# A level of a matrix inverse, copied and transposed in two halves of a PSUM pair

## The chip, the core and the metric

The kernel runs on one core of a Trainium2 chip. The metric is the device time of one execution in microseconds (us). Engines are named as in the profile: PE is TensorE (matmuls; PEld is its weight loads), DVE is VectorE, ACT is ScalarE, POOL is GpSimd, SP is SyncE, which issues all DMAs here.

## The reference

Two parts follow on each other. The first is a linear recurrence over 768 steps for 4 batches of 8 heads with 40 channels; the state of each is 40x40. Its output, with the heads laid side by side as 3072 tokens of 320 channels, is the input of a feed-forward part with 2048 inner channels.

```python
for t in range(S):
    y[:, :, t] = np.einsum('bhd,bhde->bhe', rt, state)
    Sa = np.einsum('bhde,bhe->bhd', state, at)
    state_decay = state * wt[:, :, None, :] - np.einsum('bhd,bhe->bhde', Sa, bt)
    state = state_decay + np.einsum('bhd,bhe->bhde', vt, kt)
...
h = x @ w_in
g = h * (1.0 / (1.0 + np.exp(-1.702 * h)))
return (g @ w_out).astype(np.float32)
```

All numbers are 32-bit floats.

## The kernel before

**Units.** Time is cut into 12 chunks of 64 steps, and a chunk's 32 pairs of batch and head into two units of 16; there are 24 units, two for each chunk. Within a unit the recurrence over 64 steps is solved as a triangular system: products of the inputs give score matrices (`ps_A`, `ps_N`, `ps_RV`), a triangular matrix has to be inverted (`inverse`, L662), and the inverse T is applied (`ps_X`, masked into M at L907), from which y and the next state are read (`ps_y`, L913). Two finished units of a chunk are scaled, sent through DRAM and come back as the input of the feed-forward part (`mlp`, L975: products `ps_up`, a gelu on ACT, products `ps_down`).

**Products.** Every product is a matmul with operands of 64 rows or 40 rows, on one of four 64x64 quarters of the array; four neighbours in `QUARTERS` use the four quarters. An operand of a product that many matmuls share is two PSUM banks, a pair, held as one tile of [128, 2, 512] (`psum`, L294). There are four pairs. `mm` (L299) is the line under which the profile lists all matmuls.

**The inverse.** The matrix of each head is 64x64: two diagonal blocks of 32, which are inverted by five levels of repeated squaring and multiplying, and a block below them, which is made afterwards. Units 4 to 23 use `level` (L736): a product `ps_level`, a copy of all of it to W (L751, 512 elements a partition), a subtraction (L753), a transpose (L702) and a spreading (L707, L709). Units 0 to 3 (`PLAIN`) use `plain_level` (L758): the product makes, for each of eight matrices, 96 columns, of which the first 64 are the next power and the last 32 the inverse so far. Then follow

- L784, on ACT in 15 and on DVE in one of the 16: a copy of all 2 x 4 x 96 = 768 columns of the pair to PT, the moving operand of the next level;
- L723 (called at L786), on DVE: a transpose, block by block, of the first 64 of each 96 columns to EX, the stationary operand of the next level.

The last level has 32 columns a matrix only. Behind it (the tail of the inverse):

- L790: its result is transposed into ES (L702), and ES is spread into T (L707 on ACT, in two instructions; POOL or DVE elsewhere), a tile with two places for each row block, the other filled with zeros;
- L797: eight small copies of the result into Tc, four tasks of two;
- L801, `off_one`: the product Q of P21 (the lower block of N, copied at L692) and the lower places of T; all 64 rows enter, of which the upper 32 hold zeros;
- L811: Q is masked into QT; L822, `off_two`: the product T21 of Tc and QT; L830: T21 is added to T, which is then complete for X.

**Order.** Nothing is scheduled at run time. The tasks of a plan are numbered in the order in which they are added, and a long list (`ORDER`, L107) names for every task the engine and, for those on PSUM, the pair: `300p1` is task 300 on PE with pair 1. Each engine works through its own part of the list. The semaphore waits between engines are put in by the framework from what the instructions read and write. ACT's and DVE's parts of the list also hold the conversion of the feed-forward weights (L447 on ACT, L451, L455 and L459 on DVE, L463 on POOL), which arrive as 64-bit integers' bits and fill the first 100 us or so.

Units 0 and 1 are inverted in turn between about 14 and 42 us, units 2 and 3 between about 47 and 90 us.

Of the kernel before, what the change touches and what calls it, by code (L numbers as in the profile page):

```python
# [111 lines left out]
279d 63s 280g 119p3 277s 171d1 36s 44s 123a3 120d3 343s 125d3 121a 278g 124d3 29d 287a 126p2 170a1 288p0 127a2 30d 172p1 122a3
31d 289a0 128p2 54s 173a1 129d2 32g 174d1 134p3 147s 37a 290d0 175p2 135d3 180a2 146s 178a2 275s 176d2 136p1 179a2 479s 38d
181a2 45s 39d 177a 282g 291d 91s 138a1 182p0 188p3 281d 183a0 186p2 139d 137a1 283p0 187a2 184p1 189a3 40d 276s 292p2 46a
284d0 41g 285p3 185d1 344s 148a 286d3 190p0 293a2 294d2 334p1 335p3 357a 140s 191d0 268g 336a3 315d 192p2 47d 337a1 348d 316p0
194a2 295p3 349d 61s 317a0 195g 60s 347s 358p1 296a3 62s 297d3 360d1 318a0 298p3 271a 361d 319p0 338g 300d3 196s 193a2 320a0
346s 355p2 385d 270s 48d 299a3 362p0 356d2 351g 301p3 363a0 364d0 350g 269s 141s 386p2 197s 302d3 365p0 387a2 352g 359a1 303d3
388a2 323p1 367d0 366a0 321p3 49d 324a1 304p2 322a3 478s 325d1 50g 353p0 309a2 470p3 354d0 209p1 307a2 210p1 310a2 305d2 211p1
308a2 272d 198p0 341a 199p0 72s 212p1 70s 64a 200p0 340s 368p2 52s 342d 339s 69s 201p0 369a2 202p0 370d2 203p0 471a 213p1 65d
214p1 389p2 66d 472a3 483g 204p0 390a2 560s 371p3 67d 306a 53s 215p1 71s 482s 216p1 372a3 217p1 476a 220p2 373d3 68g 218p1  # L120
221p2 477d 219a1 205p0 222p2 206p0 223p2 224p2 207p0 55a 311p3 225p2 79s 312d3 80s 226p2 208a0 58d 313p1 374p3 314d1 227p2 56d
379a3 228p2 229p2 57d 326p0 230a2 59g 393p1 327d0 378a3 391p2 394a1 375d3 231p0 558s 392d2 376a 232p0 233p0 395d1 559s 81s 73a
78s 234p0 480s 381p2 235p0 328p1 481s 382a2 74d 377a3 485d 380a3 236p0 75d 492a 242p2 486d 243p2 82a 76d 484d 77g 383p3 237p0
384d3 244p2 329d1 330d1 488p3 473d 238p0 531d 245p2 487g 246p2 489d3 85d 532p1 239p0 533a1 396p3 331d 332s 474s 475s 534a1
240p0 247p2 397d3 562s 241a0 535p1 83d 490p3 536a1 84d 398p0 572a 491d3 86g 550p1 555s 561s 253p3 399d0 551a 333s 400d0 254p3
401d 402s 554s 255p3 552a1 564d 493p0 705s 556a 567g 570p1 403s 494d0 248p2 563d 566g 249p2 495d0 498d 256p3 571d1 565g 250a2
496a0 251d2 252s 696p1 497g 557d 539p0 537p2 704s 257p3 538a2 540d0 258p3 553d 611d 697a 499d 573p2 784s 700s 259p3 576a2
574d2 710d 260p3 541d0 575d2 404p0 578d 261a3 577g 405p0 579d 698a1 568p2 711g 500p1 406p0 569d2 501a1 407p0 262d3 263s 708s
580p2 702a 502d1 408p0 582d2 409p0 503d 410p0 583d 504a 612p3 411p0 584g 613d3 412p0 614d3 413p0 505p1 709d 414a0 426p3 506d1
427p3 428p3 507d1 429p3 699d 581d2 430p3 615p1 785s 706s 701s 703d 431p3 616a1 585p0 432p3 508d 586a0 433p3 587d0 434p3 509a  # L130
588d 435p3 589d 448p2 436a3 510p1 590p0 511a1 449p2 592d0 591a0 512d1 415p3 513d 416p3 593d 514a 417p3 594g 418p3 515p0 419p3
516a0 517d0 595p1 518d 420p3 596a1 597d1 421p3 598d 422p3 519a 599d 423p3 424p3 520p0 425a3 437p1 521d0 438p1 523d0 522g 439p1
524d0 440p1 525d0 441p1 442p1 526d0 527p3 718p0 929s 528a3 443p1 719d0 787s 444p1 720d0 529p3 445p1 721d0 446p1 530d3 600p0
723d 447a1 542p3 722d 724g 603d0 605a0 619p1 604d0 543d3 450p2 620a1 606d0 544p3 621d1 601d0 602d 617p1 707s 546d3 451p2 618a1
783s 712d 547g 713d 607p0 725p1 608a0 452p2 609p0 453p2 548s 610d0 932s 454p2 727d1 726d1 622p0 728d 545d3 729a 775p1 455p2
623d0 780s 776a 549s 756d 730p3 624p0 456d2 457d2 731d3 458s 459p2 777a1 778g 732d3 786s 788g 781a 779s 626d0 460p2 625d0 627g
733d 795p1 835d 734a 461p2 735p3 791g 462p2 628s 736a3 796d1 737d3 716p0 792g 738d 463p2 782d 739g 1011s 920p1 757p3 925s
464p2 717d0 758a3 629s 759a3 790d 465p2 740p0 789d 466p2 741a0 742d0 921a 797p3 467d2 760p0 1008s 468d2 800a3 923d 652p2 469s
761d0 922a1 653p2 926a 930s 798d3 714p1 799d3 654p2 924s 802d 801g 655p2 934d 803a 656p2 836p0 657p2 715d1 658p2 659p2 837d0
762p3 838d0 927d 660p2 763a3 661p2 764p1 662a2 743d 630p0 744d 928s 631p0 632p0 765d1 804p3 766d1 633p0 805a3 806d3 634p0 807d  # L140
635p0 808a 745p2 636p0 748d2 637p0 749d2 839p1 933g 750d2 638p0 840a1 1009s 751d2 639p0 809p3 746d2 935g 640a0 641p1 810d3
642p1 793p2 747a 811d3 674p0 812d 794d2 813a 752p3 643p1 753a3 814p2 644p1 815a2 816d2 754p3 645p1 755d3 646p1 817d 647p1 818a
767p2 841p3 768d2 648p1 842a3 649p1 819p2 650p1 820a2 821d2 675p0 769p3 822d 651a1 823d 771d3 931s 770d3 772g 824p2 936d 676p0
827a2 828a2 942p1 829a2 677p0 1153s 830a2 937d 945a1 773s 663p3 825d2 664p3 943d1 1156s 826a 665p3 944d1 999p2 947d 946g 666p3
1000a 1004s 980d 940p1 948g 667p3 941d1 668p3 774s 669p3 670p3 831p1 671p3 1001a2 1002d 1003s 832d1 672p3 1005a 1013d 678p0
673a3 1006d 833p2 843p1 679p0 834d2 1007s 844d1 938p2 845d1 680p0 939d2 846p3 681p0 847d3 949p1 1012g 682d0 848p2 950a1 683d0
1014d 684s 685p3 849d2 1015g 1010s 850d2 1021p0 1016g 951d1 686p3 1024a0 1232s 851d 1235s 981p2 687p3 982a2 952d 852s 1022d0
983a2 953g 1144p1 1023d0 688p3 1026d 1145a 1149s 1025d 1027g 984p2 1059d 689p3 1154s 954p0 853s 985a2 1147g 690p3 1158d 1148s
955a0 956d0 986p2 1146a1 957d 1150a 691p3 958d 987a2 1151d 988p0 692p3 989a0 1152s 990d0 959p1 693a3 865p2 960a1 694d3 866p2
961d1 867p2 695s 962d 868p2 963d 1028p0 869p2 1029a0 1030d0 870p2 1031d 1157g 871p2 1159d 1032a 1060p3 872p2 873p2 1061a3  # L150
874p2 1062d3 1033p1 875a2 854p0 1035d1 855p0 1036d 856p0 1037d 1063p3 857p0 1064d3 1034a1 858p0 964p2 859p0 965a2 966d2 1038p1
967d 860p0 1039a1 1040d1 861p0 1041d 1017p3 968a 1042g 862p0 1018d3 863p0 969p2 864a0 876p1 970d2 877p1 972d2 971g 1043p3
973d2 878p1 1044a3 974d2 879p1 975d2 880p1 881p1 1045d3 1019p0 1046d 976p2 1047a 882p1 1020d0 1233s 883p1 977a2 1166p3 884p1
1169a3 1167d3 1377s 978p0 885p1 1168d3 898p2 1171d 1170g 886a1 979d0 887p3 1172a 1048p0 991p1 1051a0 888p3 1052a0 992d1 889p3
1053a0 890p3 1054a0 891p3 1049d0 993p1 1050a 1067p0 994d1 1160g 1155s 892p3 1161d 1068a0 893p3 894p3 1069d0 1380s 895p3 1204d
1065p0 995d1 896p3 996d 1066a0 1231s 1055p1 899p2 897a3 1056d1 997s 1173p0 1223p3 900p2 1174a0 1175d0 1228s 1176d 1224a 1177g
1057p1 901p2 1058d1 1070p0 998s 1164p1 1225a3 1226d 1236g 1227s 1071d0 902p2 1229a 1165d1 1162p3 903p2 1238d 1163d3 904p2
1237d 1178p0 1230d 905p2 1179a0 1180d0 1245p1 906a2 1181d 1072p3 1248a1 1456s 907d2 1182g 1246d1 908s 1247d1 909p0 1250d 1234s
1239g 1073d3 1251a 910p0 1240g 1074d3 1249d 1183p2 1459s 1283d 1368p1 911p0 1184a2 1075d 1373s 912p0 1185d2 1369a 1076s 1186d
1252p3 1187d 913p0 1370a1 1371g 1372s 1382d 1253a3 1188p2 1254d3 1374a 914p0 1255d 1190d2 1256g 1077s 1189a2 1191d 1243p1  # L160
1375d 915p0 1192g 1257p3 916p0 1244d1 1258a3 1259d3 1205p2 917d0 1206a2 1193p1 918d0 1207a2 1089p3 1260d 919s 1196a1 1090p3
# [87 lines left out]
def rwkv7_gelu_quick(ctx: ExitStack, tc: tile.TileContext, time_d, v_d, w_d, wc_d, ak_d, b_d, rv_d, w_in, w_out, out):  # L249
    nc = tc.nc  # L250
# [407 lines left out]
    def turn(i, n, of):  # L658
        return of * 2 * (i // 2) + i % 2 + 2 * n
# [470 lines left out]
```

## Time and profile before

| what | value |
|---|---|
| median of 3 runs | 678.3 us (677.63 to 680.24) |
| the profiled execution | 678.87 us |
| its span in the trace | 677.2 us |
| granted PE clock over the span | 0.989 |
| L784 on ACT (768 elements) | 15 times, 800 ns |
| L723 from PSUM (512 elements) | 16 times, 709 ns |
| L751 on ACT (512 elements) | 56 times, 585 ns |
| matmuls of Q | 384 in the trace (two for each), 220 ns |

The span runs from the first to the last instruction; the execution's own time has a little around it. A row of a group gives how often an instruction stands in the trace, its busy time, the mean of one in ns, and the idle time of its engine just before it with what ended that idle time. A matmul's own duration is its way through the array; neighbours overlap, so that a block of 16 takes far less than 16 durations.

### The profile page before, as it was taken

Reading aid. Unit: us, or ns where it says so; the run is one execution under the profiler, and the core shown is the slowest. Engines: PE = TensorE matmul, PEld = TensorE weight load, DVE = VectorE, ACT = ScalarE, POOL = GpSimd, SP = SyncE. Lnnn points to the kernel's source line nnn. Section 1 sums busy time; section 2 is a strip of 40 time slices with the busy share of each in tenths; the row PEclk is TensorE's granted clock in tenths of the full one; section 3 lists DMA queues with packets and bytes.
Section 4 is the critical chain, followed back from the end, with each engine's and each line's share of the span. In section 5 each row is a group of like instructions: output and inputs, shape, how many; then the busy total and the mean of one; then the engine's idle time right before and its main releaser. Section 6 shows DMA issues by size and latency. Waiting matters only on the chain.

```text
span 677.2 us, 42176 instructions
## 1 busy us (share of the span) xinstructions
PE 650.6 (96%) x19488; PEld 561.3 (83%) x19488; DVE 447.1 (66%) x906; ACT 330.6 (49%) x688; POOL 175.0 (26%) x204
## 2 busy tenths in 40 slices
PE   5668999999999999999999999999999999999997
PEld 5567887987987888898998898787988799899895
DVE  5686887777768668667776687868556766675001
ACT  4675955634664655554545435454454354252110
POOL 6442444224123023124123211321412321300000
PEclk9887999999999999999999999999999999999999
DMA  7883736315324224332304413513412412100100
GB/s 234 295 252 126 235 111 183 103 45 157 111 64 132 84 62 129 106 107 77 113 24 133 139 34 108 155 33 107 145 34 72 126 46 63 53 14 29 45 12 20
DMA packets 35311, 69.72 MB, mean 103 GB/s; under 512 B 5440, under 2 KB 14656, under 8 KB 35136
## 3 DMA queue, kind: packets, MB, share of 16 engines
q1 hardware_dynamic: 35136, 67.03, 32.6%
q8 instruction: 153, 2.51, 1.5%
q14 instruction: 22, 0.18, 0.1%
HBM read 59.15 MB, written 7.86 MB: 99 GB/s over the span
## 4 chain that ended last, share of the span: by engine, by line
PE 94%; ACT 2%; DVE 2%; issue 1%; DMA 1%; DVEq 0%; ACTq 0%; SPq 0%
PE ps_up L300 31%; PE ps_down L300 31%; PE ps_level L300 9%; PE ps_y L300 5%; PE ps_B L300 5%; PE ps_X L300 2%; PE ps_A L300 2%; PE ps_rz L300 2%; PE ps_N L300 2%; PE ps_RV L300 2%; PE ps_zT L300 1%; ACT PT L784 1%; PE ps_cum L300 1%; PE ps_Q L300 1%; PE ps_T L300 1%
## 5 line engine op out<-in xcount | busy, mean ns | idle before, releaser
L300 PE MATMUL ps_up<-xT_all,w_sb 64*64 64x256 f32 x3840 | 250.1, 377 | 0.4 <-PE ps_rz L300 0.2
L300 PE MATMUL ps_down<-w_sb,g 64*64 64x320 f32 x3072 | 239.5, 430 | 0.3 <-ACT zr L869 0.2
L300 PEld LDWEIGHTS ps_up<-xT_all,w_sb 64*64 64x64 f32 x3840 | 169.6, 133 | 15.3 <-issue 0.8
L300 PEld LDWEIGHTS ps_down<-w_sb,g 64*64 64x64 f32 x3072 | 133.3, 133 | 39.8 <-issue 1.3
L988 ACT ACTIVATE g<-ps_up 128x1024 f32<-128x1024 f32 x48 | 49.2, 1024 | 45.0 <-PE ps_up L300 44.6
L709 POOL TENSOR_TENSOR EX<-ES,quads 128x512 f32<-128x512 f32 x29 | 38.3, 1323 | 113.3 <-DVE ES L702 75.8
L751 ACT COPY W<-ps_level 128x512 f32<-128x512 f32 x56 | 32.7, 585 | 69.7 <-PE ps_level L300 68.0
L300 PEld LDWEIGHTS ps_level<-W,EX 64*64 64x64 f32 x2560 | 58.7, 134 | 5.8 <-DVE T L830 0.2
L300 PE MATMUL ps_level<-W,EX 64*64 64x64 f32 (+1 forms) x2560 | 55.9, 217 | 0.0
L753 DVE TENSOR_TENSOR E<-two,ps_level 128x256 f32<-128x256 f32 x80 | 33.2, 416 | 34.0 <-ACT W L751 30.3
L707 ACT ACTIVATE EX<-ES,quads 128x256 f32<-128x256 f32 x80 | 36.3, 501 | 30.5 <-DVE ES L702 29.9
L619 POOL TENSOR_TENSOR ak<-ak,FT 128x512 f32<-128x512 f32 x16 | 21.4, 1335 | 75.9 <-DMA ak<-in_ak 52.0
L300 PEld LDWEIGHTS ps_level<-PT,EX 64*64 64x64 f32 x1280 | 32.1, 146 | 8.8 <-DVE EX L723 5.7
L300 PE MATMUL ps_level<-PT,EX 64*64 64x64 f32 (+2 forms) x1280 | 34.2, 245 | 5.3 <-DVE EX L723 4.5
L702 DVE STREAM_TRANSPOSE ES<-E 128x256 f32<-128x256 f32 x80 | 35.3, 443 | 4.4
L300 PE MATMUL ps_y<-M,bh 64*64 64x104 f32 (+1 forms) x768 | 35.0, 247 | 2.4 <-issue 2.1
L300 PE MATMUL ps_y<-RV,kh 64*64 64x104 f32 (+1 forms) x768 | 34.8, 247 | 0.0
L891 ACT COPY B<-ps_B 128x416 f32<-128x416 f32 (+1 forms) x34 | 16.5, 491 | 33.8 <-PE ps_B L300 33.6
L300 PEld LDWEIGHTS ps_y<-RV,kh 64*64 64x64 f32 x768 | 28.5, 133 | 2.3 <-DVE M L907 0.5
L300 PEld LDWEIGHTS ps_y<-M,bh 64*64 64x64 f32 x768 | 27.2, 133 | 2.8 <-issue 2.3
L907 DVE TENSOR_TENSOR M<-ps_X,later 128x832 f32<-128x832 f32 (+1 forms) x24 | 23.8, 993 | 8.2 <-PE ps_X L300 8.0
L627 POOL TENSOR_TENSOR kh<-time,G 128x320 f32<-128x320 f32 x18 | 16.1, 892 | 48.5 <-PE ps_y L300 34.6
(131 smaller groups left out, 1092.9 us busy)
## 6 DMA issues: line engine op xcount, KB each, us to landing
ak<-in_ak SPq DMA_DIRECT2D x48, 160.0 KB
rv<-in_rv SPq DMA_DIRECT2D x48, 160.0 KB
time<-in_time SPq DMA_DIRECT2D x24, 320.0 KB
xT_all<-x_dram SPq DMA_DIRECT2D x48, 160.0 KB
wc<-in_wc SPq DMA_DIRECT2D x20, 264.0 KB
logw<-in_w SPq DMA_DIRECT2D x24, 160.0 KB
RV<-in_v SPq DMA_DIRECT2D x24, 160.0 KB
b<-in_b SPq DMA_DIRECT2D x48, 80.0 KB
```

The lines of the kernel that those rows point to most:

```text
L300: nc.tensor.matmul(o, lhsT, rhs, start=start, stop=True, skip_group_check=True)
L619: plan.add(R, {"DVE": 690.0, "POOL": 1270.0, "sbuf": True}, lambda t: of(t.engine).tensor_mul(ahT(), ahT(), FT_of(i)), reads=T("ak", "FT") ...
L627: plan.add(R + 4, {"POOL": 870.0, "DVE": 490.0, "sbuf": True}, lambda t, n=n, dst=dst: of(t.engine).tensor_mul(dst(i)[:, :, :D], by_head(t ...
L702: plan.add(rank, dve(256), lambda t: nc.vector.transpose(ES(n), source(t)), writes=[key("ES", n, 6)], **reads)
L707: nc.scalar.activation(dst[:, :, h], ES(n), ACT.Copy, scale=quads[:, h, :1])
L709: of(t.engine).tensor_mul(dst, ES(n).unsqueeze(2).to_broadcast([128, 8, 2, 32]), quads.unsqueeze(1).to_broadcast([128, 8, 2, 32]))
L751: plan.add(rank, any2(512), lambda t: copy(t.engine)(tiles_of(W(n + 1)), blocks(psum(t, ""), 64)), writes=[key("W", n + 1, 5)], pair=pair)
L753: plan.add(rank, dve(256), lambda t: nc.vector.tensor_sub(tiles_of(E(n + 1)), every(two32, [128, 2, 4, 32]), blocks(psum(t, ""), 64)[:, :, ...
L784: plan.add(rank, any2(768), lambda t: copy(t.engine)(tiles_of(PT), blocks(psum(t, ""), 96)), writes=[("PV", turn(i, n + 1, 5))], pair=pair)
L891: plan.add(R, any2(4 * wide), lambda t: copy(t.engine)(dst(), some(psum(t, "")[:, :, :208])), writes=[("Bv", i)] if x and c > 0 else T("B" ...
L907: plan.add(R + 1, dve(8 * wide), lambda t: nc.vector.tensor_tensor(M_of(i)[:, :, :wide].rearrange("p (j b) n -> p b j n", b=2), some(psum( ...
L988: plan.add(-45, {"ACT": 1030.0, "table": "gelu"}, lambda t: nc.scalar.activation(g_of(c * NQ + q).rearrange("p m r n -> p r m n"), psum(t, ...
```

## The change

- **Halves.** In `plain_level` the copy of 768 becomes two of 384, one for each bank of the pair (`copied(r)`), and the transpose of 512 two of 256 (`transposed(r)`). They are added in the order: copy of bank 1, transpose of bank 0, transpose of bank 1, copy of bank 0.
- **Trimmed copies.** The last level reads only the last 32 columns of each matrix. The copy ahead of it leaves the others out: 2 x 128 elements instead of 768 in `plain_level`, 256 instead of 512 at L751 (once in each of units 4 to 23).
- **32-row product.** Q reads ES and the lower 32 of each 64 rows of P21, instead of the lower places of T and all 64 rows. It waits for the transpose L702 and no longer for the spreading of T. The tile of its matmuls in the built program is 32x64 instead of 64x64; that of all others stays 64x64.
- **Order.** `ORDER` is written anew for the 32 tasks more. In the built program the instructions of SP and POOL stand as before. On PE only two things differ: the source of Q, and in unit 0 the product N of unit 2, which stood behind Q and now stands behind T21. On ACT the four Tc copies on ACT in unit 0's tail now all stand ahead of QT, and QT ahead of the spreading of T (before: two Tc copies, T, preset, a copy of unit 1, QT, two Tc copies). Some results of units 1 and 2, which DVE transposed ahead of ACT's copy (among them the first of unit 1), now have their copy of bank 1 first. On DVE only the pairs of halves are new.

```diff
+    LOWER = [slice(h.start + 32, h.stop) for h in HALF]
...
-            plan.add(rank, any2(512), lambda t: copy(t.engine)(tiles_of(W(n + 1)), blocks(psum(t, ""), 64)),
+            past = 32 if n == LEVELS - 2 else 0
+            plan.add(rank, any2(512 - 8 * past), lambda t: copy(t.engine)(tiles_of(W(n + 1))[:, :, :, past:], blocks(psum(t, ""), 64)[:, :, :, past:]),
...
-            plan.add(rank, any2(768), lambda t: copy(t.engine)(tiles_of(PT), blocks(psum(t, ""), 96)),
-                     writes=[("PV", turn(i, n + 1, 5))], pair=pair)
-            turned_square(lambda t: blocks(psum(t, ""), 96)[:, :, :, :64], dict(pair=pair), n + 1)
+            past = 64 if n == LEVELS - 2 else 0
+
+            def copied(r):
+                plan.add(rank, any2(384 - 4 * past), lambda t: copy(t.engine)(tiles_of(PT)[:, r, :, past:], blocks(psum(t, ""), 96)[:, r, :, past:]),
+                         writes=[("PV", turn(i, n + 1, 5))], pair=pair)
+
+            def transposed(r):
+                plan.add(rank + 0.5, dve(256), lambda t: nc.vector.transpose(tiles_of(square(n + 1))[:, r], blocks(psum(t, ""), 96)[:, r, :, :64]),
+                         writes=[key("EX", n + 1, 5)], pair=pair)
+            copied(1)
+            transposed(0)
+            transposed(1)
+            copied(0)
...
-                    mm(ps[HALF[u], b, e * 64:e * 64 + 64].rearrange("p (f t) -> p f t", f=2), at(P21_t, i)[HALF[b], 128 * e + 64 * u:128 * e + 64 * u + 64],
-                       at(T_t, i)[HALF[b], j:j + 2, 1], e == 0)
-        plan.add(R + 3.5, pe((2, 64)), off_one, reads=T("P21", "T0"), room=T("QT"), pair=("Q", i))
+                    mm(ps[HALF[u], b, e * 64:e * 64 + 64].rearrange("p (f t) -> p f t", f=2), at(P21_t, i)[LOWER[b], 128 * e + 64 * u:128 * e + 64 * u + 64],
+                       ES(LEVELS)[LOWER[b], j:j + 2], e == 0)
+        plan.add(R + 3.5, pe((2, 64)), off_one, reads=T("P21") + [key("ES", LEVELS, 6)], room=T("QT"), pair=("Q", i))
```

More of the change, by code (lines that the diff above doesn't have):

```diff
@@ L112 @@
[L112 to L115, printed above, removed]
@@ new lines @@
+2606p1 2291p0 2545d3 2546d 2607d1 2547a 2292p0 2548p2 2293a0 2617p3 2549a2 2294d0 2452p1 2618d3 2453p1 2295s 2454p1 2550d2
+2649p0 2551d 2455p1 2650a0 2619d3 2552g 2456p1 2651a0 2620d 2457p1 2621a 2652p2 2458p1 2653d2 2553p3 2459p1 2554a3 2555d3
+2460p1 2556d 2461p1 2557d 2622p0 2462a1 2463p2 2623d0 2464p2 2465p2 2624d0 2558p3 2625d 2466p2 2626d 2559a3 2467p2 2560d3
+2468p2 2561d 2469p2 2562a 2627p0 2470p2 2628d0 2471p2 2472p2 2629d0 2563p1 2630d 2473a2 2474p3 2631d 2475p3 2564d1 2476p3
+2566d1 2565a 2632p0 2567d1 2477p3 2478p3 2568d1 2633a0 2479p3 2569d1 2480p3 2634d0 2570p2 2635d 2481p3 2636d 2571a2 2482p3
@@ L245 @@
+2513p1 2676a3 2514p1 2677p2 2515a1 2678p2 2516d1 2710p0 2517s 2679p2 2680p2 2681p2 2682p2 2683p2 2684p2 2685p2 2686p2 2711p0
+2687a2 2688p3 2689p3 2690p3 2691p3 2692p3 2693p3 2694p3 2695p3 2696p3 2697p3 2712p0 2698a3 2699p1 2700p1 2701p1 2702p1 2703p1
+2704p1 2705p1 2706p1 2707p1 2708p1 2713p0 2709a1 2714p0 2715p0 2716p0 2717p0 2721p2 2718d0 2719d0 2722p2 2720s 2723p2 2724p2
+2725p2 2726p2 2727p2 2728p2 2729d2 2730d2 2731s
 """
```

263 lines of the change are left out of this document (130 added, 133 removed).

## The prediction

> **What bounds the kernel now.** I read the page first, then the busy time by stage, then the chain that ended last.
>
> ```profile
> span 677.2 us, 42176 instructions
> ...
> PE 650.6 (96%) x19488; PEld 561.3 (83%) x19488; DVE 447.1 (66%) x906; ACT 330.6 (49%) x688; POOL 175.0 (26%) x204
> ```
> ```profile
> 17.04:42.30 25.26, 16.20 (x605) 13.89 (x605) 19.25 (x32) 17.75 (x43) 11.34 (x7) 0.93 0.90 295
> 42.30:69.76 27.46, 22.96 (x863) 21.89 (x867) 18.32 (x31) 16.51 (x40) 10.22 (x12) 0.81 0.48 147
> 69.76:626.00 556.24, 555.41 (x17029) 478.25 (x17026) 397.50 (x823) 284.48 (x577) 142.89 (x144) 1.00 0.32 95
> ```
>
> The columns of the second view are the stretch, its length, the busy time of PE, PE's weight loads, DVE, ACT and POOL, the granted clock, the DMA share and GB/s. From 69.76 us on PE is idle for 556.24 - 555.41 = 0.83 us in 556: there PE bounds the kernel, in a fixed order, so a delay that exists at 69.76 us reaches the end whole, and a faster ACT or DVE gives nothing. Only the stretches before that have room: PE idles 9.06 us in the first and 4.50 us in the second, and the clock is cut in both. The first four units, whose levels the change rewrites, have nearly all of them there. Which wait ends last in these stretches, the chain of waits says (start, length, what):
>
> ```profile
> 18.64 1.15 PE ps_level L300 x40
> ...
> 19.87 0.81 ACT PT L784
> ...
> 20.70 0.73 DVE EX L723
> ...
> 21.48 2.03 PE ps_level L300 x40
> ...
> 34.13 0.91 ACT T L707 x2
> ...
> 39.36 1.02 DVE M L907
> ...
> 40.43 0.40 PE ps_y L300 x5
> 40.82 2.07 issue
> ```
>
> The reader sees a level: PE's product ends at 19.79, ACT copies it (0.81), only then DVE transposes it (0.73), only then PE goes on, at 21.48. From product to product that is 1.69 us. ACT and DVE both merely read the same PSUM pair, and still one waits for the other.
>
> **The change part by part.** By its form, ACT would copy bank 1 while DVE transposes bank 0, and then the reverse. I looked in the built program at what each instruction waits for. In every level whose copy ACT makes it is: copy of bank 1; transpose of bank 0, **waiting for that copy**; transpose of bank 1; copy of bank 0, **waiting for both transposes**; and PE's next product waits for this last copy. So nothing runs crosswise, and I price four steps in a row.
>
> ```profile
> L784 ACT COPY PT<-ps_level 128x768 f32<-128x768 f32 x15 | 12.0, 800 | 7.2 <-PE ps_level L300 5.1 <-ACT wch L569 1.0 <-DVE EX L723 0.9
> L692 ACT COPY P<-ps_N 128x256 f32<-128x256 f32 x22 | 8.2, 371 | 23.1 <-PE ps_N L300 21.6 <-DVE PT L716 1.0 <-DVE PT L689 0.3
> L702 DVE STREAM_TRANSPOSE ES<-ps_level 128x256 f32<-128x256 f32 x24 | 10.7, 445 | 7.0 <-PE ps_level L300 4.1 <-ACT Tc L797 2.6
> ```
> ```profile
> 24.27 1.37 ACT L447 ACTIVATE w_sb<-extra 128x1280 f32<-128x1280 f32 x1
> ...
> 24.41 1.31 DVE L723 STREAM_TRANSPOSE EX<-ps_level 128x512 f32<-128x512 f32 x2 [1.29 <-ACT PT L784]
> ...
> 26.61 0.89 PE L300 MATMUL ps_level<-PT,EX 64*64 64x96 f32 x32 [0.73 <-ACT PT L784]
> ...
> 27.84 0.80 ACT L784 COPY PT<-ps_level 128x768 f32<-128x768 f32 x1
> ...
> 29.44 0.89 PE L300 MATMUL ps_level<-PT,EX 64*64 64x96 f32 x32 [0.76 <-DVE EX L723]
> ...
> 35.09 0.46 PE L300 MATMUL ps_Q<-T,P 64*64 64x64 f32 x16 [1.96 <-ACT T L707]
> ...
> 38.12 0.94 PE L300 MATMUL ps_X<-B,T 64*64 64x104 f32 x32 [0.69 <-DVE T L830]
> ```
> ```profile
> L797 ACT COPY Tc<-ps_level 32x64 f32<-32x64 f32 x88 | 17.7, 202 | 11.2 <-PE ps_level L300 8.5 <-DVE ES L702 1.6
> ...
> L816 ACT ACTIVATE QT<-ps_Q,quads 128x128 f32<-128x128 f32 x36 | 11.2, 362 | 16.3 <-PE ps_Q L300 15.1 <-PE ps_zT L300 1.1
> ...
> L455 DVE TENSOR_SCALAR w_sb<-w_sb 128x1280 int32<-128x1280 int32 x8 | 6.6, 825 | 0.2
> ...
> L404 ACT COPY PT<-one 128x256 f32<-128x256 f32 x8 | 3.2, 423 | 0.0
> ...
> L716 DVE TENSOR_TENSOR PT<-ps_N,within 128x512 f32<-128x512 f32 x4 | 2.6, 662 | 1.2 <-ACT P L692 1.2
> ```
>
> Copies of 768 and 256 elements take 800 and 371 ns, 0.84 ns an element, so 384 take 0.48 us, and 128 (the trimmed copies of the fourth level) an estimated 0.26. Two transposes of 256 take 2 x 0.445 less the 0.07 or so by which neighbours on DVE overlap (the two at 24.41 take 1.31 together, the singles 0.73): 0.82. A full level is then 0.08 + 0.48 + 0.02 + 0.82 + 0.03 + 0.48 + 0.04 = 1.95 us instead of 1.69, **0.26 more**; the fourth is 1.51, 0.18 less. ACT now waits in the middle of each level, and what stands behind the waiting copy in its queue (the weight conversions of L447, G, P) waits with it, and after that DVE's conversions and masks, which take those. I walk the first stretch by the built order, units 0 and 1 in turn; neighbours on one engine overlap by up to 0.1, as in the rows.
>
> - Unit 0's second and third level products start at 18.64 + 0.26 = 18.90 and 21.48 + 0.52 = 22.00. The third runs at half clock until 23.7 (the window is quoted below) and ends at 23.9, and its second half-copy at 25.8.
> - Next on ACT stands the weight conversion of 24.27, now until 27.1. Before, DVE transposed unit 1's first result during this conversion (the second one of the pair at 24.41), and only the copy stood behind it. Now unit 1's first half-copy stands behind the conversion and all else behind that copy: 27.1 + 0.48 + 0.02 + 0.82 + 0.03 + 0.48 + 0.04 = 28.97 where PE had started at 26.61: **+2.4**.
> - ACT's exponentials follow as before, so the copy of 27.84 starts at 30.2 and ends as a half at 30.7. DVE has three conversions of 0.82 until 30.85, then both transposes until 31.7; the last half-copy ends at 32.15. PE's next product (29.44) waits for it: 32.2, **+2.8**.
> - The trimmed level gives 0.1 back, and Q no longer waits for the 0.91 us of T. But its source is transposed behind unit 1's two halves, at 36.5 to 36.9: Q moves from 35.09 to 36.95, +1.9. ACT then has four Tc copies behind DVE's four (eight of 0.2: 38.7), QT (two of 0.36: 39.4) and only then T (0.91: until 40.2). The sum at L830 needs T, and X after it moves from 38.12 to 40.7, **+2.6**.
> - M stands on DVE behind unit 1's two transposes and unit 2's mask, and the mask behind ACT's copy of P: unit 1's trimmed level ends at 41.8, the preset (0.42, less overlap) and P (0.37) at 42.4, the mask (0.66) at 43.0. M runs from there instead of 39.36, and y's products that wait for it start at 44.05 instead of 40.43: **+3.6**.
>
> Then comes a gap of 2.07 us within y, for which the profile shows no releaser. If it runs beside PE's longer wait for M, y resumes at 44.05, 1.2 behind the old 42.89; if it follows that wait, 3.6 behind. I take the middle, +2.4. The second stretch has one level bare on the chain, and one product of unit 3 to watch:
>
> ```profile
> 56.70 0.81 ACT PT L784
> ...
> 57.53 0.73 DVE EX L723
> ...
> 58.30 1.98 PE ps_level L300 x40
> ...
> 65.50 1.11 PE ps_level L300 x40
> ```
>
> The bare level adds 0.26. Between 62 and 69 us DVE and ACT serve units 2 and 3 in turn; ahead of the product at 65.50 DVE now has a mask and both halves where it had one transpose in time. By the same adding it comes at 66.4, +0.9. Together 2.4 + 0.26 + 0.9 = **+3.55 us** at 69.76, bounded by +1.2 (the gap hidden, the other two covered) and +4.8. The DMA issues and POOL's instructions stand in the same order as before, and none is passed. Behind 69.76 the halved W copies of 20 units and the earlier Q are off the path: PE has feed-forward products between all steps, and they give and cost nothing.
>
> What remains is the **32-row product**: 24 blocks of Q, 22 of them in the PE-bound part. No row shows a product of 32 rows among those of 64.
>
> ```profile
> 82.61 0.44 PE L300 MATMUL ps_Q<-T,P 64*64 64x64 f32 x16
> ...
> 82.84 1.07 PE L300 MATMUL ps_up<-xT_all,w_sb 64*64 64x256 f32 x16
> ```
> ```profile
> L300 PE MATMUL ps_up<-xT_all,w_sb 64*64 64x256 f32 x3840 | 250.1, 377 | 0.4 <-PE ps_rz L300 0.2 <-issue 0.2
> ...
> L300 PEld LDWEIGHTS ps_up<-xT_all,w_sb 64*64 64x64 f32 x3840 | 169.6, 133 | 15.3 <-issue 0.8 <-DVE B L894 0.5 <-PE ps_rz L300 0.3
> ...
> L300 PEld LDWEIGHTS ps_B<-zr,ak 40*64 40x64 f32 x704 | 19.9, 133 | 0.3 <-issue 0.3
> ...
> L300 PE MATMUL ps_Q<-T,P 64*64 64x64 f32 x384 | 11.3, 220 | 2.0 <-ACT T L707 2.0
> ```
>
> A block of Q takes 82.84 - 82.61 = 0.23 us of PE. Fewer rows save nothing (a weight load of 40 rows takes 133 ns, as one of 64), so the cost isn't below zero. At the top, PE would let the product before (377 ns) and Q (220 ns) run out and load the first weights bare on both sides (2 x 133): 0.86 us a block. I take 0.05, near the row in which Q follows up without a gap: 22 x 0.05 = **1.1 us**; the ends are 0 and 19. The Trainium skill, "TensorEngine Tiling (Array Packing)", Key Properties, says that a change of the tiling mode, not merely of the tile, drains the engine; all products of before have one tile form, so no row here shows it. By that rule rival B's term would stand in place of the 1.1.
>
> Sum: the profiled execution took 678.87 us (the span and 1.6 around it). 678.87 + 3.55 + 1.1 = 683.5; it lies 0.57 above the median of the runs shown (678.3), so **683.0 us** in medians.
>
> **The rivals.**
> - *B, the product drains PE.* For it: tiles of another height amid the rest. Against it: nothing in this trace. Without the bare loads a block costs what is left of the product before (377 less its pace, 250.1 us / 3840 = 65 ns) and of Q (220 less 14): 0.52 us, and 22 x 0.52 = 11.4 in place of 1.1 makes 693.3. Between 0.1 and 0.52 a block it is 684 to 693.
> - *C, no change: the clock.* It stood at half in windows that followed on idle PE, such as
>
> ```profile
> 16.90:20.30 3.40, 1.70 (x78) 1.52 (x79) 1.41 (x2) 1.64 (x3) 1.79 (x2) 1.00 0.97 337
> 20.30:23.70 3.40, 3.33 (x97) 3.14 (x90) 2.38 (x4) 1.57 (x5) 0.86 (x1) 0.50 0.83 284
> ```
>
>   In the second stretch the clock of 0.81 costs up to 0.19 x 27.46 = 5.2 us. If the delays shift PE's idle time so that each window holds more than the 1.70 us busy of the first row, that comes back: 683.0 - 5.2 = 677.8. Against it: a longer chain makes more idle time, which can as well halve another window (up to +1.7).
> - *D, faster: the halves do run crosswise.* Then a level is 0.08 + 0.48 + 0.03 + 0.48 + 0.04 = 1.11, 0.58 less, on some eight levels of the chain 4.6, and T's 0.91 leaves it too: 678.3 - 5.5 = 672.8. The point that decides is whether DVE's first transpose starts before ACT's first half-copy ends. Against it stand the waits of the built program, which put it behind.
>
> **How the numbers follow.** Forecast 0.42 (its own range 680 to 685), B 0.28, C 0.17, D 0.13. About 0.5%, 3.4 us, is what a measurement of this kernel can tell from no change; the bounds are 674.9 and 681.7. Faster: D, 0.13. Same: C and the part of the forecast in which the gap is hidden, 0.17 + 0.07 = 0.24. Slower: the rest of it and B, 0.35 + 0.28 = 0.63. The range leaves out D and the upper end of B: 676.5 to 692.5.
>
> **What would show it.** In the chain of waits before 42 us a level shows ACT, DVE twice, ACT, one behind the other; the product of 26.61 starts near 29, M near 43; T no longer stands ahead of Q. Behind 70 us, idle PE in front of Q or of the product behind it tells B from the forecast. The forecast is wrong if a transpose overlaps a copy of its level, if fewer windows are at half clock, or if Q's blocks show gaps.

## The result, and the profile after

| | before | after |
|---|---|---|
| median of 4 runs | 678.95 us (677.63 to 680.24) | 689.4 us (687.44 to 690.55) |
| the profiled execution | 678.87 us | 689.98 us |
| its span | 677.2 us | 688.3 us |
| granted PE clock over the span | 0.989 | 0.979 |

The changed kernel takes 1.0157 of the time before (95% interval 1.013 to 1.0185): 10.45 us more by the medians, 11.1 in the profiled executions. The forecast was 683.0 us, range 676.5 to 692.5: the side was right and the range holds the time, but the rise is more than twice the 4.7 us that were forecast.

The page of after, and its busy time in the three stretches that the prediction showed of before (stretch, its length, then PE, weight loads, DVE, ACT, POOL, granted clock, DMA share, GB/s):

```profile
span 688.3 us, 42217 instructions
...
PE 660.7 (96%) x19488; PEld 519.2 (75%) x19488; DVE 444.4 (65%) x923; ACT 328.4 (48%) x703; POOL 174.9 (25%) x204
```
```profile
17.11:44.50 27.39, 19.64 (x593) 17.83 (x597) 18.42 (x37) 16.20 (x42) 10.64 (x7) 0.69 0.86 274
44.50:74.65 30.15, 23.41 (x877) 21.27 (x875) 19.76 (x41) 18.80 (x53) 9.71 (x12) 0.83 0.43 134
74.65:626.00 551.35, 550.44 (x16684) 434.87 (x16679) 390.49 (x814) 279.14 (x575) 143.72 (x144) 1.00 0.32 95
```

PE is counted 10.1 us busier for the same 19488 products, and the weight loads 42 us less busy. The first product of the feed-forward part (below: the first `ps_up`) starts at 74.65 us; in before it starts at 69.59 (the block that the chain shows from 69.76). So **5.1 us are lost ahead of it and 6.05 behind it**: 688.3 - 74.65 = 613.65 against 677.2 - 69.59 = 607.6. The forecast had 3.55 and 1.1.

**Behind it.** PE, and then the weight loads, around the first block of Q behind the first `ps_up` of after (start, time to the last end, what; in brackets the idle time ahead):

```profile
88.59 0.46 PE L303 MATMUL ps_Q<-ES,P 32*64 32x64 f32 x16
88.98 1.09 PE L303 MATMUL ps_up<-xT_all,w_sb 64*64 64x256 f32 x16
```
```profile
87.40 0.80 PEld L303 LDWEIGHTS ps_up<-xT_all,w_sb 64*64 64x64 f32 x16
88.58 0.32 PEld L303 LDWEIGHTS ps_Q<-ES,P 32*64 32x64 f32 x16 [0.38 <-ACT g L1002]
88.98 0.64 PEld L303 LDWEIGHTS ps_up<-xT_all,w_sb 64*64 64x64 f32 x16
```

The same weight loads of before, at the block of 82.61:

```profile
82.40 0.52 PEld L300 LDWEIGHTS ps_Q<-T,P 64*64 64x64 f32 x16
82.79 0.67 PEld L300 LDWEIGHTS ps_up<-xT_all,w_sb 64*64 64x64 f32 x16
```

In before, Q's first weights load 0.21 us ahead of its first product (82.40 and 82.61), while the products before still run, and the next block's weights load while Q runs. In after the loads stand still for 0.38 us and begin 0.01 us ahead of Q's first product; the next block's weights, too, begin only with its first product (88.98). From Q's start to the next product it is 0.39 us in each of the 22 blocks; in before it is 0.23 in most. The row of the group shows the same (idle time behind the second bar); first after, then before:

```profile
L303 PEld LDWEIGHTS ps_Q<-ES,P 32*64 32x64 f32 x384 | 7.9, 135 | 9.3 <-issue 4.9 <-DVE ES L705 1.0 <-ACT g L1002 0.9
```
```profile
L300 PEld LDWEIGHTS ps_Q<-T,P 64*64 64x64 f32 x384 | 11.7, 135 | 3.8 <-ACT T L707 2.2 <-issue 0.2
```

**Ahead of it.** The chain that ended last in after, at unit 1's first levels (start, length, what):

```profile
23.21 4.04 DMA w_sb<-in_w_in
27.25 0.41 DVE EX L795
...
27.68 0.49 ACT PT L791
...
28.21 2.03 PE ps_level L303 x40
...
30.32 0.49 ACT PT L791
...
30.83 0.79 DVE EX L795 x2
...
31.70 0.49 ACT PT L791
...
32.23 2.03 PE ps_level L303 x40
...
37.84 0.71 PE ps_Q L303 x16
...
41.94 1.50 PE ps_X L303 x32
```

ACT, DVE twice, ACT, one behind the other: from 30.24 to 32.23 PE waits 1.99 us. And both products of 2.03 us ran at half clock (a granted clock of 0.50). The half-clock stretches of after, then those of before behind the one that the prediction quoted:

```profile
27.50:44.57 17.07, 14.61 (x372) 13.37 (x376) 12.65 (x26) 10.38 (x30) 8.36 (x4) 0.50 0.81 248
...
58.22:68.46 10.24, 8.72 (x236) 8.31 (x239) 3.91 (x9) 4.83 (x11) 2.91 (x4) 0.50 0.48 142
```
```profile
44.20:47.60 3.40, 3.31 (x103) 3.13 (x99) 2.58 (x7) 2.79 (x7) 1.50 (x2) 0.50 0.41 127
...
57.84:64.67 6.83, 6.37 (x172) 6.33 (x176) 4.12 (x7) 3.59 (x7) 1.96 (x2) 0.50 0.65 203
```

27.3 us at half clock, against 3.4 + 3.4 + 6.8 = 13.6. These are one execution of each kernel. In the second profiled execution of each (e11 and e5 below) the clock, read in steps of 0.5 us up to 76 us, adds up to 23.9 us at half clock in both; so the difference can't be put down to the change.

### The profile page after: what moved, and what is told of

Read it like the earlier page. It is cut to its first block, busy times and chain, and to the rows that moved or that the text cites. A ratio compares the mean times of both kernels' runs of the same rounds, so it can differ in the third digit from the quotient of the medians.

```text
span 688.3 us, 42217 instructions
## 1 busy us (share of the span) xinstructions
PE 660.7 (96%) x19488; PEld 519.2 (75%) x19488; DVE 444.4 (65%) x923; ACT 328.4 (48%) x703; POOL 174.9 (25%) x204
## 3 DMA queue, kind: packets, MB, share of 16 engines
q1 hardware_dynamic: 35136, 67.03, 32.2%
## 4 chain that ended last, share of the span: by engine, by line
PE 92%; DVE 3%; ACT 2%; DMA 1%; issue 1%; SPq 0%; ACTq 0%; DVEq 0%
PE ps_down L303 30%; PE ps_up L303 30%; PE ps_level L303 9%; PE ps_y L303 5%; PE ps_B L303 5%; PE ps_X L303 3%; PE ps_N L303 2%; PE ps_rz L303 2%; PE ps_A L303 1%; PE ps_RV L303 1%; PE ps_Q L303 1%; PE ps_zT L303 1%; PE ps_cum L303 1%; ACT PT L791 1%; DVE EX L795 1%
## 5 line engine op out<-in xcount | busy, mean ns | idle before, releaser
L303 PE MATMUL ps_up<-xT_all,w_sb 64*64 64x256 f32 x3840 | 244.9, 378 | 0.2 <-PE ps_rz L303 0.2
L303 PE MATMUL ps_down<-w_sb,g 64*64 64x320 f32 x3072 | 233.9, 430 | 0.2 <-ACT zr L883 0.2
L303 PEld LDWEIGHTS ps_up<-xT_all,w_sb 64*64 64x64 f32 x3840 | 149.8, 134 | 30.1 <-DVE B L908 0.5
L303 PEld LDWEIGHTS ps_down<-w_sb,g 64*64 64x64 f32 x3072 | 112.0, 133 | 56.5 <-ACT zr L883 0.4
L755 ACT COPY W<-ps_level 128x512 f32<-128x512 f32 (+1 forms) x56 | 29.5, 527 | 69.6 <-PE ps_level L303 67.9
L303 PEld LDWEIGHTS ps_level<-W,EX 64*64 64x64 f32 x2560 | 55.3, 135 | 8.1 <-DVE T L844 0.2
L303 PE MATMUL ps_level<-W,EX 64*64 64x64 f32 (+1 forms) x2560 | 53.1, 218 | 0.0
L303 PE MATMUL ps_level<-PT,EX 64*64 64x64 f32 (+2 forms) x1280 | 36.4, 258 | 8.7 <-ACT PT L791 8.3
L921 DVE TENSOR_TENSOR M<-ps_X,later 128x832 f32<-128x832 f32 (+1 forms) x24 | 23.9, 994 | 8.8 <-PE ps_X L303 8.5
L692 DVE COPY_PREDICATED PT<-within,ps_N 128x256 f32<-128x256 uint32 x40 | 17.7, 444 | 17.2 <-ACT P L695 11.5
L303 PEld LDWEIGHTS ps_y<-RV,kh 64*64 64x64 f32 x768 | 24.4, 134 | 3.6 <-DVE M L921 0.5
```

The costliest lines, as they stand in the source:

```text
L303: nc.tensor.matmul(o, lhsT, rhs, start=start, stop=True, skip_group_check=True)
L692: plan.add(R, dve(256), lambda t, n=n: nc.vector.copy_predicated(tiles_of(at(E0_t, i)), every(within_of(n), [128, 2, 4, 32]), blocks(psum( ...
L755: plan.add(rank, any2(512 - 8 * past), lambda t: copy(t.engine)(tiles_of(W(n + 1))[:, :, :, past:], blocks(psum(t, ""), 64)[:, :, :, past: ...
L921: plan.add(R + 1, dve(8 * wide), lambda t: nc.vector.tensor_tensor(M_of(i)[:, :, :wide].rearrange("p (j b) n -> p b j n", b=2), some(psum( ...
```

## The experiments

Theory 1: a block of 32-row products amid products of 64 rows costs PE time where the form changes, and this is what is lost behind 74.65 us. Theory 2: the halves, kept in a row by two waits (of a transpose for the copy of the other bank, and of the last copy for both transposes), make the early part longer, that is, the time up to the first `ps_up`. Rivals: the new order of ACT's work in unit 0's tail (below: the tail order) or the trimmed copies are the cause. Each run is compared with the kernel before on the same chip; four chips took part, with medians of before from 677.0 to 681.6 us.

### The 32-row product

**The product alone, in the kernel before** (e1):

```
-  at(P21_t, i)[HALF[b], 128 * e + 64 * u:128 * e + 64 * u + 64], at(T_t, i)[HALF[b], j:j + 2, 1]
+  at(P21_t, i)[LOWER[b], 128 * e + 64 * u:128 * e + 64 * u + 64], at(T_t, i)[LOWER[b], j:j + 2, 1]
```

> Only Q of the kernel before is changed: its products read rows 32 to 63 of each half of P21 and T instead of all 64 (the rows left out are zero in T). Order, copies and transposes are those of before. Theory 1 (each block of 32-row products costs PE time at both of its ends; in the changed kernel a block of Q took 0.39 us to the next product instead of 0.23, and 0.54 instead of about 0.43 stood ahead of it): about 0.27 us for each of the 22 blocks behind 69.6 us, +5.9 us: a profiled execution of 684 to 685.5, the first product of the feed-forward part at 69.6 as before. The forecast on record (0.05 a block): 680. Rival (the blocks cost nothing, and what the changed kernel loses behind 74.65 us comes from its order): 679.

Measured: 683.95 us against 677.04, ratio 1.0128 (1.008 to 1.0176); profiled execution 684.67, first `ps_up` at 70.4. The last two blocks of Q, of before (with one in the middle of its span) and of this kernel:

```profile
252.84 0.65 PE L300 MATMUL ps_up<-xT_all,w_sb 64*64 64x256 f32 x8
253.28 0.45 PE L300 MATMUL ps_Q<-T,P 64*64 64x64 f32 x16
...
609.62 0.42 PE L300 MATMUL ps_Q<-T,P 64*64 64x64 f32 x14
...
616.27 0.42 PE L300 MATMUL ps_Q<-T,P 64*64 64x64 f32 x14
```
```profile
614.94 0.46 PE L301 MATMUL ps_Q<-T,P 32*64 32x64 f32 x16
...
621.37 0.61 PE L301 MATMUL ps_up<-xT_all,w_sb 64*64 64x256 f32 x8
621.91 0.46 PE L301 MATMUL ps_Q<-T,P 32*64 32x64 f32 x16
622.30 0.45 PE L301 MATMUL ps_up<-xT_all,w_sb 64*64 64x256 f32 x4
```

From block to block it is 6.97 us instead of 6.65: 0.32 more. Over the 21 stretches between the 22 blocks the median is **0.31 us a block**, here as in the changed kernel: 0.16 behind Q's start (0.39 less 0.23), most of the rest ahead of it (from the eight `ps_up` instructions to Q's start it is 0.54; in before 0.44, 252.84 to 253.28). 22 x 0.31 = 6.8 us. Single stretches scatter: those of after are from 0.41 us shorter to 0.52 longer than those of before, 4.97 in all, and those of e1 4.73. By the profiles, the time behind the first `ps_up` is 5.0 to 7.5 us longer than in before where all 22 blocks have 32 rows (e1 and e4 5.0 and 5.1, e3 and after 6.0, e5 7.5), and it differs by 2.3 us between two executions of before itself (607.6 and, in e11, 609.9). So 6.8 is a median, not known to the last microsecond; e1's time agrees with it (6.9).

**64 rows again in units 4 to 23 of the changed kernel** (e2):

```
-  at(P21_t, i)[LOWER[b], ...], ES(LEVELS)[LOWER[b], j:j + 2]
+  at(P21_t, i)[(LOWER if i < PLAIN else HALF)[b], ...],
+  ES(LEVELS)[LOWER[b], j:j + 2] if i < PLAIN else at(T_t, i)[HALF[b], j:j + 2, 1]
```

> The changed kernel, with Q of units 4 to 23 on 64 rows again (from T, which their order has ready); units 0 to 3 keep the 32 rows. Theory 1: 20 blocks by 0.27 us go: 5.4 less than the changed kernel, a profiled execution near 684.6; the stretch before the first feed-forward product stays as it is, 74.65 us. Rival (the later part is lost to the order or to ACT's and DVE's halves): 689 to 690, with the blocks at 0.23 us all the same.

Measured: 682.61 against 677.04, 1.0101 (1.0068 to 1.0134). Most of the 20 blocks take 0.23 us again, the median stretch between them is that of before to 0.01 us, and the two blocks that kept 32 rows still take 0.39. The first `ps_up` came at 70.42, though, not at 74.65: that figure is not the code's own (e5).

**Each block twice** (e8): `lambda t: (off_one(t), off_one(t))` in place of `off_one`.

> The changed kernel with each block of Q done twice in place, the second time over the same result (32 of 32-row products instead of 16 in a trace's count, output unchanged). Theory 1 (the cost is at the two changes of form): a block grows by what 64-row products of the same number take, 0.23 us, from 0.39 to about 0.62 until the next product, 22 x 0.23 = 5 us in all. Rival (each product of 32 rows is slower by itself): it grows by 0.39 or more, to 0.78, 8.6 us in all.

```profile
87.29 0.69 PE L303 MATMUL ps_Q<-ES,P 32*64 32x64 f32 x32
87.91 1.09 PE L303 MATMUL ps_up<-xT_all,w_sb 64*64 64x256 f32 x16
```

0.62 us for twice the products, as theory 1 has it: among themselves, 32-row products run at the pace of 64-row ones. The stretch from block to block is 0.55 longer than before's (0.31 and 0.23); the time is 698.71 against 680.31, 1.0258 (1.0207 to 1.0308).

**One product of 32 rows ahead of the 64-row block, in the kernel before** (b1):

```
+  low = slice(32, 64)
+  mm(ps[HALF[0], 0, :64].rearrange("p (f t) -> p f t", f=2), at(P21_t, i)[low, :64], at(T_t, i)[low, :2, 1], True)
   for e in BITS:
```

> The kernel before with one product of 32 rows (two instructions in the trace) put ahead of each of the 24 blocks of Q, into a place that the block's first product of 64 rows then overwrites; the result stays. Theory (the cost hangs on the change of form, once per block): nearly the whole 0.31 us a block for one product, 22 x (0.31 + 0.03) = 7.5 us over before, with the idle time of the weight loads around it. Rival (it goes with the number of 32-row products): 2/16 of 0.31, with its own time 0.07 a block, 1.5 us.

```profile
624.11 0.61 PE L300 MATMUL ps_up<-xT_all,w_sb 64*64 64x256 f32 x8
624.65 0.71 PE L300 MATMUL ps_Q<-T,P 32*64 32x64 f32 x18
625.18 1.05 PE L300 MATMUL ps_up<-xT_all,w_sb 64*64 64x256 f32 x16
```

690.5 us against 681.56, 1.0139 (1.0096 to 1.0183): as much as the whole block. Again 0.54 us stand ahead of Q, and the block takes 0.53 to the next product instead of 0.23; from block to block 0.41 more (median). So the cost hangs on the change of form, there and back, and hardly on how many products have it.

### The halves

**The changed kernel on another chip** (e5, no edit):

> The changed kernel as it is, beside the next three on one chip, because the first feed-forward product came at 74.65 us in its profiled execution and at 70.42 in that of the kernel with the 64-row Q, whose first four units are the same code. If 74.65 is the code's own: 74 to 75 again, and the time 1.5% over that of the kernel before. If it is the course of one execution (which stretches ran at half clock, when the weights landed): near 70.5, and about 6.8 (22 blocks by 0.31, which is what the stretches from Q to Q have become longer by) and 1 over the profiled execution of before.

Measured: 691.04 against 680.31, 1.0145 (1.0112 to 1.0178). First `ps_up` at 73.0 us, between the two figures that were expected (74 to 75, and 70.5).

**The halves alone, in the kernel before and its order** (e9):

```
-  plan.add(rank, any2(768), lambda t: copy(t.engine)(tiles_of(PT), blocks(psum(t, ""), 96)), ...)
-  turned_square(lambda t: blocks(psum(t, ""), 96)[:, :, :, :64], dict(pair=pair), n + 1)
+  # copy of bank 1 at the copy's place; transposes of banks 0, 1 and copy of bank 0 at the transpose's
```

> The kernel before with the halves alone, in its own order: copy of bank 1, transposes of banks 0 and 1, copy of bank 0, with the waits that put them in a row. Q, tail order and untrimmed copies stay as before. The forecast's term for the halves: +2.4 to +3.6 us at the first feed-forward product, 1 to 5 in all, and nothing behind it; level steps of 1.95 us. Rival (early delays are taken up by DMA waits and half-clock stretches that come anyway): within 1 us of before. The two kernels that differ in the halves alone and the changed kernel gave 1.8 us (691.0 less 683.1, of which 6.2 are 20 blocks of Q), so 1 to 3 is the likeliest.

Measured: 687.25 against 681.2, 1.0093 (1.0059 to 1.0127), first `ps_up` at 72.9. Behind it the profile took 611.9 us, where the two executions of before took 607.6 and 609.9; why, the runs do not show. Its chain at two products for which the prediction's walk gave 28.97 and 32.2:

```profile
28.46 1.86 PE ps_level L300 x40
...
30.40 0.49 ACT PT L789
30.91 0.79 DVE EX L791 x2
...
31.78 0.49 ACT PT L789
...
32.31 2.03 PE ps_level L300 x40
```

**The two waits taken off** (e4 in the changed kernel; e7 with 64 rows in units 4 to 23 besides; e10 in the kernel before, PT's copies trimmed). Each half waits for the product and for the other engine's read of its own bank alone:

```
+  for other, bank, old in readers.setdefault(t.pair, []):
+      if other != what and bank != r:
+          tc.declare_no_dep(inst.ins, old.ins, reason="reads of two banks")
```

> The changed kernel, with the two waits taken off that put a half-transpose behind the half-copy of the other bank and the last half-copy behind both transposes: each half now waits for the product and for the other engine's read of its own bank only. What is computed is unchanged. Rival D of the record (the halves can run side by side): a level step of about 1.1 us instead of 1.95, the first feed-forward product at 66 to 71 us, the whole at 680 to 686, and the 32-row blocks still cost their 5.9. Against it (two engines that read one PSUM pair hold each other up, or PE's wait for both banks eats it): half-copies of more than 0.55 us or half-transposes of more than 0.5, a level step of 1.6 or more, and 687 to 690.

> The changed kernel with both mends: the halves truly side by side, and 64 rows in Q of units 4 to 23. Theory: the later part as fast as before or up to 1.4 us faster, the blocks' 0.31 gone but for two; the early part, whose level step fell from 1.95 to 1.2 us (58.85 to 60.04) without the first feed-forward product coming earlier than 70.3, is set by DVE's weight conversions and half-clock stretches: 676 to 679, level with before. If the halves do shorten the chain: 671 to 675. If the tail order costs: 680 to 682.

> The kernel before with halves that run side by side (waits on the own bank alone) and PT copies trimmed at the fourth level, in its own order, with Q as before: what the change could have been. A level step of about 1.2 us instead of 1.69. If the chain of copies and transposes sets the early part, some eight steps by 0.5: 2 to 4 us below before. If DVE's weight conversions, the landing of the weights and the half-clock stretches set it: within 1 us of before.

The chain of e4, at the level that the prediction called bare in the second stretch:

```profile
57.99 0.87 PE ps_level L303 x19
...
58.93 0.49 ACT PT L798
...
59.44 0.46 DVE EX L802
...
60.04 0.96 PE ps_level L303 x18
```

The copy of bank 1, then the transpose of that bank, then PE: from 58.85 to 60.04, 1.2 us instead of 2.0, and neither half got longer than in a row. Yet: e4 684.73 against 677.04, 1.0134 (1.0084 to 1.0183); e7 682.46 against 680.31, 1.0026 (0.9995 to 1.0056); e10 683.31 against 681.2, 1.0026 (0.9992 to 1.0061). The first `ps_up` comes at 70.3, 67.9 and 69.9. What stands in a level's place in the chain of e10:

```profile
22.61 0.55 ACT PT L789 x2
...
23.47 1.38 ACT w_sb L447
24.85 0.38 ACT PT L789
...
25.62 0.79 DVE extra L459
26.41 0.74 DVE w_sb L451
...
27.18 0.83 DVE w_sb L455
28.00 0.37 DVE EX L791
...
28.45 0.49 ACT PT L789
...
28.98 2.62 PE ps_level L300 x54
```

Half-copies and half-transposes stand in the queues of ACT and DVE with a weight conversion between them: ACT's of 1.38 us and three of DVE's, 2.36 together. PE starts at 28.98, in before at 26.61. There the length of a copy is not what the level waits for.

**The halves undone, the rest of the change kept** (e3; e6 with 64 rows in units 4 to 23 besides; b2 as e6, untrimmed copies besides): the first half-copy and the first half-transpose take both banks, and the second ones do nothing.

```
-  copy(t.engine)(tiles_of(PT)[:, r, :, past:], blocks(psum(t, ""), 96)[:, r, :, past:])
+  copy(t.engine)(tiles_of(PT)[:, :, :, past:], blocks(psum(t, ""), 96)[:, :, :, past:]) if r == 1 else None
-  nc.vector.transpose(tiles_of(square(n + 1))[:, r], blocks(psum(t, ""), 96)[:, r, :, :64])
+  nc.vector.transpose(tiles_of(square(n + 1)), blocks(psum(t, ""), 96)[:, :, :, :64]) if r == 0 else None
```

> The changed kernel with its halves undone: one copy of both banks, then one transpose of both, at the places of the first half-copy and the first half-transpose in the order. Trimmed copies, 32-row product and tail order stay. Theory 2 (the four steps in a row make the early part longer): the level step is 1.69 us again instead of 1.95, and the first feed-forward product comes back from 74.65 to between 69.6 and 71, the whole to 684.5 to 686. Rival (the new tail order, with T's spread behind Tc and QT, or the trimmed copies, cause it): 74 to 75 and 689 to 690. If the half-clock windows follow their own course, it is anything between, and the windows' rows must tell.

> The changed kernel with 64 rows in Q of units 4 to 23 and with the halves undone: what is left against the kernel before are trimmed copies, 32 rows in the first four units and the tail order. Theory (the halves in a row cost the early part 1 to 3 us, tail order and trimmed copies nothing): 1 to 3 us below the next kernel's counterpart with serial halves (682.6 against 677.0 before), so 0 to +3 against before. Rival (the tail order is the cost): +5 as with the halves.

> The changed kernel without its halves, without the trimmed copies and with 64 rows in Q of units 4 to 23: against before, the tail order and the early source of Q in units 0 to 3 are left (and 32 rows there: 2 of the 22 blocks, 0.6 us). If the tail order costs what the kernel without halves kept (683.1 against 680.3): +2 to +4, more than that one, which had trimmed copies (-1.2 alone). If the tail order is free: +0.6, and the 2 was scatter.

Measured: e3 686.33 against 677.04, 1.0145 (1.0112 to 1.0178), first `ps_up` at 68.2; e6 683.06 against 680.31, 1.0018 (0.9991 to 1.0046); b2 683.65 against 681.56, 1.0037 (1.0011 to 1.0063).

**The trimmed copies alone**, in the kernel before (e12, and once more as b3):

```
+  past = 64 if n == LEVELS - 2 else 0
-  copy(t.engine)(tiles_of(PT), blocks(psum(t, ""), 96))
+  copy(t.engine)(tiles_of(PT)[:, :, :, past:], blocks(psum(t, ""), 96)[:, :, :, past:])
   # and W's copy likewise with past = 32
```

> The kernel before with the trimmed copies alone (W's and PT's copies into the last level take only the columns that it reads). The forecast: a fourth level shorter by 0.3 us or so in the first stretch, nothing behind; within 0.7 us of before. Rival (fewer elements written let ACT run ahead and its other work collide with DVE's or PE's): a difference of over 1 us either way.

> The kernel with the trimmed copies alone, as run before (0.9984 of before, 0.9961 to 1.0007), again. If it is a gain: 0.998 again, the two together below 1. If not: 0.999 to 1.002.

Measured: 0.9984 (0.9961 to 1.0007) and 0.9996 (0.9965 to 1.0027): no change that can be told.

**The kernel before, a second profile** (e11, no edit):

> The kernel before unchanged, for a second profiled execution: the first feed-forward product between 69 and 71 us, and 588.3 us from it to the last one's start but for stalls; whether the half-clock stretches lie where they lay (20.3, 44.2 and 57.8 us) or move from one execution to the next.

683.82 us in its one run; first `ps_up` at 72.3, 2.7 us later than in the first profile of the same code. Most of one long stretch ran at half clock, where the first profile had full clock but for 3.4 us:

```profile
31.50:52.00 20.50, 16.77 (x505) 15.55 (x501) 13.57 (x26) 12.21 (x32) 8.28 (x5) 0.58 0.68 216
```

**Taken together.** The first `ps_up` of all 17 profiles tells how long the early part was. In the five with halves in a row (after, e5, e8, e9, e2) it came at 74.65, 73.0, 73.3, 72.9 and 70.4 us, in the mean at 72.9; in the twelve others between 67.9 and 72.3, in the mean at 69.6. That is 3.3 us in the mean, though e2 lies among the others. The three with halves side by side have 69.4 in the mean, the three with the tail order and no halves (68.2, 71.1 and 70.5) 69.9, the six with neither 69.5: no early cost of the tail order can be told.

The times give a second count. The difference of the medians, less 0.31 us for each 32-row block behind the first `ps_up` (22, or 2 where units 4 to 23 have 64 rows; 0.55 a block for e8 and 0.41 for b1), leaves:

| what else differs from before | us over before that are left |
|---|---|
| halves in a row: after, e5, e2, e9, e8 | 3.65, 3.9, 5.0, 6.05, 6.3 |
| halves side by side: e4, e7, e10 | 0.9, 1.5, 2.1 |
| no halves, the rest of the change: e3, e6, b2 | 2.5, 2.1, 1.5 |
| product alone: e1, b1; trimmed copies alone: e12, b3 | 0.1, -0.1; -1.2, -1.6 |

A ratio's interval is about 0.3% on either side, 2 us, and more for the runs with few executions, so neighbours in this table can't be told apart. What is left need not lie in the early part: see e9 above, and the profile of b2, one of its longest executions, which took 6.8 us more than before behind the first `ps_up`. The first group stands above the rest: with the two waits it is 2.4 to 4.1 us more than without (e2 to e4, e5 to e7, and e9 to e10, which also trims a copy). Undoing the halves in the changed kernel gave back only 1.2 and 1.8 us (after to e3, e5 to e6), no more than the noise. How much the tail order costs, whether the 1.5 to 2.5 us of the third group are its price, stays open. No version was found that beats the kernel before; that with trimmed copies alone is level with it.

## Why the prediction was wrong in size, and right elsewhere

- *The 32-row product: this step failed.* The prediction put 1.1 us, 0.05 a block, "near the row in which Q follows up without a gap". That row shows a block of 64 rows among products of 64 rows, and so says nothing of a change of form. Measured: 0.31 a block, 6.8 us. With it the sum is 678.87 + 3.55 + 6.8 - 0.57 = 688.65, 0.75 below the measured 689.4; that it comes so close is in part luck, as single executions of one kernel differ by several us.
- *Rival B had the mechanism, at too high a price.* It let the product before and Q run out in full, 0.52 a block, 11.4 us. Measured were 0.10 to 0.14 ahead and 0.16 behind Q's start, and no weights load ahead across the change (88.58 and 88.98). The rows do not show PE empty at the change: in e1 Q starts at 621.91, 0.07 us before the last `ps_up` ahead of it ends (621.37 + 0.61), though ends of matmuls are modelled in the profile. Why it is 0.31 and not 0.52 stays open. The Trainium skill, "TensorEngine Tiling (Array Packing)", Key Properties, says that a change of the tiling mode drains the engine. The runs agree that the change costs time, 0.31 us there and back (e1, e8, b1); how far the engine empties, no run here shows.
- *Where B would show.* The prediction looked for idle PE around Q. There is none: 551.35 - 550.44 = 0.91 us idle behind 74.65, as before. The lost time counts as busy PE; the sign is idle time of the weight loads ahead of Q (0.38 us), and times from start to start.
- *The halves in a row: right.* Four steps of 0.49, 0.79 for two, and 0.49, where 0.48, 0.82 and 0.48 were forecast, a step of 1.99 (1.95). (The prediction took 0.07 off for the overlap of two transposes; the rows that it names, 2 x 0.73 less 1.31, give 0.15, and 2 x 0.445 less 0.79 is 0.10.) The walk gave 28.97, 32.2, 36.95 (Q) and 40.7 (X); after has 28.21, 32.23, 37.84 and 41.94. The first came earlier, released by a DVE step behind a landing weight DMA that the walk didn't have; Q and X were late by 0.9 and 1.2, with 17 us at half clock on the way.
- *The early part: right in sum, 3.55 us for 3.3* (the means of the first `ps_up` above; 3.65 by the medians of the times). A single pair of profiles says little: 5.1 here, 0.7 between e5 and e11. The walk behind X was less good. In after M starts at 43.98 and the products of y that wait for it at 45.05, each 1.0 us later than forecast; the products that before had at 55.63, 58.30 and 65.50 came 3.3, 4.4 and 4.9 us later, where the walk had 2.4, 2.7 and 3.55. Half clock accounts for part of it, as the first of the three took 1.78 us instead of 0.99. By the times, the halves alone cost 6.05 (e9), more than the walk gave them; how far the tail order adds to it or takes from it, the runs do not settle.
- *Rival C, the clock gives it back: no.* Half clock lasted longer, 27.3 us for 13.6, in the first profiles, and as long, 23.9 us, in the second ones. *Rival D, the halves run crosswise: no, as the built waits said.* Taken off (e4), a level does take 1.2 us, but D's gain of 5.5 below before didn't come (e7, e10: 2 us over before, which can't be told from level with it): its sum took each of eight levels as bare, while in the chain of e10 weight conversions stand between the halves.
- *Trimmed copies, with the halved W copies behind 70 us: nothing that can be told, as forecast* (e12, b3; the median stretch of e2 equals that of before).

## What to carry to other kernels

Before products are cut to fewer rows, look whether every other product on PE has the same tile form: one product of another form cost as much here as a block of them, so keep the form and let zeros run along, as before does. To gather such products in one place would be the other way; no run here tried it. A copy cut in halves "to run crosswise" can gain only if each half waits for its own bank alone; read the waits in the built program, and then look at what stands between the halves in the engines' queues. Where no row shows an operation, a row that lacks the property in question (here, the change of form) says nothing of its price: give the mechanism's price a full share of the sum. Here 0.31 lay between the 0.05 taken and the mechanism's 0.52.

## What the runs showed of the hardware that was not expected

- A change between 64-row and 32-row tile form, there and back, costs 0.31 us on a busy PE, and the profile books it as busy: behind the first `ps_up` PE is busy for 607.87 us in after and for 601.91 in before, which is 5.96 of the 6.05 us by which this part got longer.
- With such changes the weight loads are busy for less time: 519.2 us in after, 522.4 in e5, 516.8 in e1, against 561.3 and 574.8 in the two profiles of before and 557.9 in e2 with 20 blocks on 64 rows. The mean of one stays at 133 to 135 ns, so more of them overlap; the runs do not show why.
- The half-clock stretches ahead of 75 us move from one execution of a kernel to the next: the first `ps_up` of the same code started at 69.6 and 72.3 us (before), at 74.65 and 73.0 (after), with 13.6 and 23.9, 27.3 and 23.9 us at half clock. One profile says little about single microseconds there.
